# Twelve matmuls at equal addresses instead of six, in fewer pairs, and half of the output weights' sums a chunk earlier

## The chip, the cores and the metric

The kernel runs on one core of a Trainium2 chip. A core has five engines that run at their own pace and wait for one another by semaphores: TensorE (PE, the matmuls; PEld is its loading of the stationary operand), VectorE (DVE), ScalarE (ACT), GpSimd (POOL) and SyncE (SP), which here issues nearly all transfers, in the order in which the program names them. The metric is device time in microseconds of one execution. The kernel before took 809.94 us, the median of three runs (808.45, 809.94 and 810.32).

## The reference: what is computed

Linear attention without a mask, a normalisation, and a feed-forward layer with GELU, in float32:

```python
kv = np.einsum('bhsd,bhse->bhde', k, v)            # 8 batches, 8 heads, 576 tokens, 64 dims
out = np.einsum('bhsd,bhde->bhse', q, kv)
rms = np.sqrt(np.mean(out * out, axis=-1, keepdims=True) + 1e-06)
x = out / rms * g_norm                             # then 4608 tokens x 512
h = x @ w_in                                       # 512 x 2048
g = 0.5 * h * (1.0 + erf(h / sqrt(2)))
return g @ w_out                                   # 2048 x 512
```

The precision of float32 is reached with three matmuls per product on operands split in a high and a low part: high by high, high by low, low by high.

## The kernel before, in words

**Chunks.** The 4608 tokens are done in nine chunks of 512, numbered 0 to 8. The hidden dimension of 2048 is 16 blocks, or eight pairs `j` of blocks. While a chunk's feed-forward layer runs, the attention of the next chunk (projections, line 242; the sum of squares, line 274; scaling, lines 315 and 319) and the `kv` sums of the chunk after it (line 181) are woven in.

**Three ways to do the layers.** Chunks 0 and 1 multiply plainly: `layer1` (line 678) makes a block of `h` with 12 matmuls of 512 columns, then `layer2` (line 705) adds the block of the step before to the output with 12 more. From chunk 2 on the first layer, and from chunk 3 on the second layer too, use a Strassen-Winograd scheme: of each pair of blocks seven products are made instead of eight, from operands that are sums of quarter blocks. `product` (line 539) issues one of these, six matmuls of 256 columns at line 546. So the weights are needed as *sums*, split in high and low, and these are made once, during chunks 1 and 2, and written to a scratch tensor in device memory (`products_in`, `products_out`), from which later chunks read them back.

**Where the sums are made.** Chunk 1 runs in 16 steps `i`, one block each. In steps 1 to 11 VectorE forms the sums of the input weights (`combine`, lines 416 and 433; the low parts, line 449), between its share of GELU (`rest`, line 697: the low part of the block's activation, which `layer2` of the next step needs with its third matmul). In chunk 2, which runs over the eight pairs, GpSimd forms the sums of the output weights: `sum_out(j)` issues six tensor-tensor operations (through `add`, line 537), and one pair later `split_out(j)` splits the result, with two casts on ScalarE (line 1225) and two subtractions on VectorE (line 1226). Four transfers of 256 KB then write it out (`send`). A table, `SUMS`, says at which pair which sum is made. Within a pair of chunk 2, `layer1_pair` (line 550) lets VectorE copy the first product out of PSUM after products 0 and 1 (line 562) and add it to others (line 537, operands `h` and `w_in`); product 4, the 25th matmul of the pair, writes over the same place and so waits for that copy. After the pair come 24 plain matmuls of the second layer.

**Order.** Everything stands in an order written out by hand; each engine does its own instructions in that order, and a tile's next writer waits until all its readers are done. Tiles of 4 KB per partition are handed round by name (`take` and `free`).

**Fetching and addresses.** Six tiles (`RING`: `w_in0` to `w_in3`, `w_in10`, `w_in11`) form a ring into which `fetch` reads the weights' products, 512 KB (two products) at a time. All operand tiles start at the same remainder of 256 bytes. A fetched tile is put 192 bytes further on (`AWAY`, 48 float32) so that its address differs in that remainder from the operand that it is multiplied with. There are two exceptions, at *equal* remainders: the first product of each pair of the first layer (six matmuls, the first 256 KB of the keys `("in", j, 0)`, which are therefore fetched by two transfers, line 508), and the first tick of each second layer (12 matmuls).

**The first layer of chunks 3 to 8** is a run of 336 matmuls at line 546 in this order: 24 of pair 0 (products 0 to 3), 24 of pair 1, 18 of pair 0 (products 4 to 6), 24 of pair 2, 18 of pair 1, and so on, ending with 18 of pair 7. Attention matmuls stand in it after the 18 of pair 0 and of pair 1 (projections) and of pair 2 (line 274), and up to chunk 5 `kv` sums after those of pairs 3 and 6.

Of the kernel before, what the change touches and what calls it, by code (L numbers as in the profile page):

```python
# [8 lines left out]
F32 = mybir.dt.float32  # L9
# [28 lines left out]
def linear_attn_rms_gelu_ffn(  # L38
# [453 lines left out]
    def fetch(n):  # L492

        if n < len(queue):
            key = queue[n][1]
            i = RING[n % len(RING)]
            reused(i, F32R)
            away = [0 if key == ("out", *TICKS[0]) else AWAY] * 2
            if key == ("in", key[1], 0):
                away[0] = 0  # L500
            ring[n] = [kept[i][:, a * DM + away[a]:(a + 1) * DM + away[a]] for a in range(2)]
            if away[0] == away[1]:
                to = kept[i][:, away[0]:away[0] + 2 * DM]
                nc.sync.dma_start(out=to.bitcast(F32), in_=products[key])
            else:
                for a in range(2):
                    src = products[key][:, a * DM:(a + 1) * DM]
                    nc.sync.dma_start(out=ring[n][a].bitcast(F32), in_=src)

    def operand(c, key):  # L510
        at = c, key
        if at in place:
            return ring[place[at]]
        return resident[key][:, :DM], resident[key][:, DM:2 * DM]
# [24 lines left out]
    def product(at, j, k, out, first=False):  # L539
        *key, n = place_in(j, k)  # L540
        key = tuple(key)
        w, x = operand(at.c, key)[n], at.x[k]
# [417 lines left out]
    def spread_matmuls(c, i):  # L960
# [7 lines left out]
        if c and i == 14:  # L968
            sum_kv(c + 2, range(NP))
# [29 lines left out]

    def later(c, i):  # L1000
# [20 lines left out]

    order = list(range(3, len(weights)))
# [34 lines left out]
    for s in range(PLAIN * NF):  # L1057
# [6 lines left out]
        if c and i == 15:  # L1064
            split_kv(c + 2, range(NP))
# [38 lines left out]
    class Fast:  # L1104
# [44 lines left out]
        def matmuls(self, i):  # L1149
# [7 lines left out]
            for p in range(2):  # L1157
                hi, lo = (op[:, z * CH + p * HALF:z * CH + (p + 1) * HALF] for z in range(2))
                wh, wl = (w[p][:, m * HALF:(m + 1) * HALF] for m in range(2))
# [36 lines left out]

    wide, sent = {}, []

    def sum_out(j):

        eng = nc.gpsimd
        (name, whole), (of, s) = take(), take()
        for n in range(2):
            w = parts["out", 2 * j + n].bitcast(F32)
            add(whole[:, n * DM:(n + 1) * DM], w[:, HI], w[:, LO], eng=eng)
        a11, a21, a12, a22 = (whole[:, n * HALF:(n + 1) * HALF] for n in range(4))
        s1, s2, s3, s4 = (s[:, n * HALF:(n + 1) * HALF] for n in range(4))
        for o, x, op, y in (
            (s1, a21, ALU.add, a22), (s2, s1, ALU.subtract, a11),
            (s3, a11, ALU.subtract, a21), (s4, a12, ALU.subtract, s2),  # L1210
        ):
            add(o, x, y, op, eng)
        free.append(name)
        wide[j] = of, s

    def split_out(j, places=()):
        of, s = wide.pop(j)
        s = s.rearrange("p (h k n) -> p h k n", h=2, k=2)
        for h, ks in enumerate(((1, 2), (6, 5))):
            if places:  # L1220
                slot, t = places[h], block_tile(places[h], F32R)[:, :2 * DM]
            else:
                slot, t = take(F32R)
            t = piece(t)
            nc.scalar.copy(out=t[:, :, 0], in_=s[:, h])
            nc.vector.tensor_tensor(  # L1226
# [245 lines left out]
```

## Time and profile before

The profile is of one execution. It took 808.53 us, of which 806.7 us lie between its first and its last instruction (the span).

| | busy us | share of the span | instructions |
|---|---|---|---|
| PE | 793.6 | 98% | 6248 |
| PEld | 741.2 | 92% | 6248 |
| DVE | 564.7 | 70% | 1029 |
| ACT | 369.4 | 46% | 702 |
| POOL | 207.7 | 26% | 184 |

245.4 MB moved, 304 GB/s over the span. The mean granted TensorE clock is 0.998 of full speed. "Busy" of PE includes modelled ends of matmuls that overlap the next one, so a run of matmuls is better judged by the time from one piece of the chain to the next. By the chain, chunk 1 begins near 113 us, chunk 2 at 211.3 us, chunk 3 at 307.2 us; the first layers of chunks 4 and 8 begin at 396.8 and 726.1 us. A "step" below is one of chunk 1's 16 blocks, a "pair" one of the eight pairs of blocks in the later chunks.

### The profile page before, as it was taken

To read this page: it belongs to the slowest core of one execution; us is meant where nothing else is said; L and a number is where in the kernel's file an instruction comes from. 1 tells how busy PE (TensorE), PEld (TensorE's weight loads), DVE (VectorE), ACT (ScalarE), POOL (GpSimd) and SP (SyncE) were. 2 spreads that over 40 slices of the span, in tenths; PEclk is the share of its full clock that TensorE was granted. 3 is DMA by queue.
4 is the path that set the end of the run, shared out by engine and by line. 5 is a ranking of instruction groups with operands and counts; after the bars stand their busy time and mean duration, and the time that the engine had idled before them with its cause. 6 is when DMAs were issued, how large, how long until landed. Compare 5 with 4: busy or idle time off the path is not lost.

```text
span 806.7 us, 16291 instructions
## 1 busy us (share of the span) xinstructions
PE 793.6 (98%) x6248; PEld 741.2 (92%) x6248; DVE 564.7 (70%) x1029; ACT 369.4 (46%) x702; POOL 207.7 (26%) x184
## 2 busy tenths in 40 slices
PE   8999999999999989999999999999999999999998
PEld 6688888888998879999999999999999999999997
DVE  3999757678467873769467965786479648965683
ACT  2787534434352432547154635363445443532360
POOL 1000021102345922470038002810263016201200
PEclk9999999999999999999999999999999999999999
DMA  9991317998796899999989999989899989899984
GB/s 352 407 363 53 118 41 253 357 366 292 272 333 247 307 307 354 370 373 353 366 307 347 330 370 316 350 308 301 324 315 329 322 300 308 297 327 339 329 300 163
DMA packets 98577, 245.40 MB, mean 304 GB/s; under 512 B 9924, under 2 KB 31684, under 8 KB 98500
## 3 DMA queue, kind: packets, MB, share of 16 engines
q1 hardware_dynamic: 98496, 244.36, 85.4%
q8 instruction: 50, 0.82, 0.4%
q14 instruction: 27, 0.22, 0.1%
q10 hardware_dynamic: 4, 0.00, 0.0%
HBM read 205.52 MB, written 35.13 MB: 298 GB/s over the span
## 4 chain that ended last, share of the span: by engine, by line
PE 89%; DMA 6%; DVE 3%; issue 1%; POOL 0%; SPq 0%; ACT 0%; POOLq 0%
PE acc L1163 20%; PE acc L546 17%; PE acc L705 14%; PE h L546 13%; PE h L678 10%; PE a L1163 8%; PE a L242 3%; DMA w_in<-products_in 2%; PE a L181 2%; DMA kv_tail<-kv_tail 1%; PE h L670 1%; DMA w_out<-kv_main 1%; DMA q<-qT 1%; DMA products_out<-x 1%; DVE w_out L1226 1%
## 5 line engine op out<-in xcount | busy, mean ns | idle before, releaser
L705 PE MATMUL acc<-w_out,gh 128*128 128x512 f32 x312 | 97.7, 394 | 0.0
L678 PE MATMUL h<-x,w_in 128*128 128x512 f32 x360 | 87.3, 391 | 0.0
L229 POOL TENSOR_TENSOR ql<-q,qh 128x512 fp32r<-128x512 f32 x16 | 21.5, 1347 | 246.0 <-ACT qh L228 246.0
L678 PEld LDWEIGHTS h<-x,w_in 128*128 128x128 f32 x360 | 67.5, 188 | 14.6 <-POOL x L332 0.2
L546 PE MATMUL acc<-w_out,w_in 128*128 128x256 f32 x600 | 80.0, 280 | 0.2 <-DMA w_in<-products_in 0.2
L546 PEld LDWEIGHTS acc<-w_out,w_in 128*128 128x128 f32 x600 | 73.9, 188 | 0.6 <-issue 0.4
L1163 PE MATMUL acc<-w_in,w_out 128*128 128x256 f32 x576 | 71.6, 277 | 0.0
L705 PEld LDWEIGHTS acc<-w_out,gh 128*128 128x128 f32 x312 | 57.9, 188 | 12.6
L1163 PEld LDWEIGHTS acc<-w_in,w_out 128*128 128x128 f32 x576 | 68.3, 188 | 0.0
L705 PE MATMUL acc<-w_out,gl 128*128 128x512 f32 x156 | 61.4, 393 | 0.0
L691 ACT ACTIVATE gh<-h 128x512 fp32r<-128x512 f32 x39 | 23.3, 597 | 82.9 <-PE h L678 59.2
L546 PE MATMUL acc<-x,w_in 128*128 128x256 f32 x360 | 49.4, 279 | 0.0
L546 PE MATMUL h<-w_in,w_in 128*128 128x256 f32 x312 | 42.2, 286 | 6.7 <-DVE w_in L537 6.6
L1163 PE MATMUL acc<-w_in,x 128*128 128x256 f32 x384 | 48.0, 276 | 0.0
L546 PE MATMUL h<-w_out,w_in 128*128 128x256 f32 x360 | 47.8, 279 | 0.0
L697 DVE TENSOR_TENSOR gl<-h,gh 128x512 fp32r<-128x512 f32 x39 | 26.8, 687 | 29.9 <-ACT h L692 25.7
L546 PEld LDWEIGHTS h<-w_in,w_in 128*128 128x128 f32 x312 | 39.4, 194 | 7.7 <-DVE w_in L537 7.7
L1163 PEld LDWEIGHTS acc<-w_in,x 128*128 128x128 f32 x384 | 45.7, 188 | 0.0
L546 PEld LDWEIGHTS acc<-x,w_in 128*128 128x128 f32 x360 | 45.1, 188 | 0.2
L546 PEld LDWEIGHTS h<-w_out,w_in 128*128 128x128 f32 x360 | 44.4, 188 | 0.0
L1163 PE MATMUL acc<-w_in,w_in 128*128 128x256 f32 x336 | 42.2, 277 | 0.0
L546 PE MATMUL h<-x,w_in 128*128 128x256 f32 x312 | 42.0, 279 | 0.0
(281 smaller groups left out, 1784.2 us busy)
## 6 DMA issues: line engine op xcount, KB each, us to landing
w_in<-products_out SPq DMA_DIRECT2D x126, 512.0 KB, 5.4
w_in<-products_in SPq DMA_DIRECT2D x116, 512.0 KB, 5.3
w_in<-products_in SPq DMA_DIRECT2D x112, 256.0 KB, 5.2
kv_main<-kv_main SPq DMA_DIRECT2D x22, 512.0 KB, 6.5
products_in<-w_in SPq DMA_DIRECT2D x40, 256.0 KB, 5.4
w_in<-w_in SPq DMA_DIRECT2D x16, 512.0 KB, 10.2
w_out<-w_out SPq DMA_DIRECT2D x16, 512.0 KB, 10.2
q<-qT SPq DMA_DIRECT2D x15, 512.0 KB, 6.4
```

The source lines that it names most:

```text
L181: nc.tensor.matmul(out=ps[r, n * D:(n + 1) * D], lhsT=k[:, r], rhs=v[:, r], start=(j == 0), stop=(j == NJ),)
L229: eng.tensor_tensor(out=ql, in0=q, in1=qh.bitcast(F32), op=ALU.subtract)
L242: nc.tensor.matmul(out=ps[:, a:e], lhsT=w, rhs=x[:, a:e], start=(m == 0), stop=(m == 2))
L546: nc.tensor.matmul(out=out, lhsT=y, rhs=x[:, z, kb], start=first and kb + i == 0, stop=kb == 1 and i == 2, skip_group_check=True,)
L670: nc.tensor.matmul(out=h, lhsT=ws[i].bitcast(F32)[:, p * P:(p + 1) * P], rhs=at.o_all[:, p], start=(p == 0), stop=(p == NP - 1),)
L678: nc.tensor.matmul(out=h, lhsT=parts["in", i][:, w][:, p * P:(p + 1) * P], rhs=at.x[p][:, x], start=(m + p == 0), stop=(m == 2 and p == NP ...
L691: nc.scalar.activation(out=gh, in_=h, func=AF.Gelu)
L697: nc.vector.tensor_tensor(out=gl, in0=h, in1=gh.bitcast(F32), op=ALU.subtract)
L705: nc.tensor.matmul(out=ps, lhsT=x[:, ts], rhs=parts["out", i][:, w], start=(i == 0 and m == 0), stop=(m == 2 and (i == NF - 1 or (i, t) == ...
L1163: nc.tensor.matmul(out=ps[:, a * HALF:(a + 1) * HALF], lhsT=x[:, at], rhs=y, start=(k in (0, 2, 1) and n + p + a + m == 0), stop=(n == GRO ...
L1226: nc.vector.tensor_tensor(out=t[:, :, 1], in0=s[:, h], in1=t[:, :, 0].bitcast(F32), op=ALU.subtract)
```

## The change

The change has two halves.

**Addresses.** A fetched tile now lies at equal remainders as a whole (12 matmuls, products 0 and 1) or not at all, so each is read by a single transfer. Which ones do is in a new function, `aligned`: in chunk 2 the keys `("in", j, 0)` of all eight pairs; in chunks 3 to 5 those of pairs 0, 2, 3, 4, 5; in chunks 6 and 7 of pairs 0, 2, 3, 4; in chunk 8 of pair 0 alone. The first tick of each second layer stays as it was.

**Sums.** `sum_out` and `split_out` of output pairs 0 to 3 move from chunk 2 into chunk 1: `sum_out` at steps 6, 8, 10, 12 and `split_out` and `send` one step later, in tiles named by hand. Pairs 4 to 7 stay in chunk 2, at the pairs 1, 3, 5 and 7. With it three things of chunk 1 move: the loads of `kv` from step 13 to 12, the matmuls of the `kv` sums from step 14 to 15, and their split behind step 15's second layer. The tiles that stay resident are loaded in another order (`keep`).

```diff
-            away = [0 if key == ("out", *TICKS[0]) else AWAY] * 2
-            if key == ("in", key[1], 0):
-                away[0] = 0
-            ring[n] = [kept[i][:, a * DM + away[a]:(a + 1) * DM + away[a]] for a in range(2)]
-            if away[0] == away[1]:
-                to = kept[i][:, away[0]:away[0] + 2 * DM]
-                nc.sync.dma_start(out=to.bitcast(F32), in_=products[key])
-            else:
-                for a in range(2):
-                    src = products[key][:, a * DM:(a + 1) * DM]
-                    nc.sync.dma_start(out=ring[n][a].bitcast(F32), in_=src)
+            away = 0 if aligned(*queue[n]) else AWAY
+            ring[n] = kept[i][:, away:away + 2 * DM]
+            nc.sync.dma_start(out=ring[n].bitcast(F32), in_=products[key])
+
+    def aligned(c, key):
+
+        kind, j, k = key
+        if kind == "out":
+            return (j, k) == TICKS[0]
+        if k:
+            return False
+        n = 8 if c < FAST else 6 if c + 2 < B else 5 if c + 1 < NCH else 1
+        return j < n and (c < FAST or j != 1)
...
-        if c and i == 14:
+        if c and i == 15:
             sum_kv(c + 2, range(NP))
...
+    def sum_out(j, places=()):
+
+        eng = nc.gpsimd
+        if places:
+            name = of = None
+            whole, s = (block_tile(n, F32)[:, :2 * DM] for n in places)
+        else:
+            (name, whole), (of, s) = take(), take()
+        for n in range(2):
+            w = parts["out", 2 * j + n].bitcast(F32)
+            add(whole[:, n * DM:(n + 1) * DM], w[:, HI], w[:, LO], eng=eng)
+        a11, a21, a12, a22 = (whole[:, n * HALF:(n + 1) * HALF] for n in range(4))
+        s1, s2, s3, s4 = (s[:, n * HALF:(n + 1) * HALF] for n in range(4))
+        for o, x, op, y in (
+            (s1, a21, ALU.add, a22), (s2, s1, ALU.subtract, a11),
+            (s3, a11, ALU.subtract, a21), (s4, a12, ALU.subtract, s2),
+        ):
+            add(o, x, y, op, eng)
...
-        if i == 13:
-            for p in (2, 3):
-                load_kv(c + 2, p)
         if i == 15:
+            split_kv(c + 2, range(NP))
             attn[c + 2].load(1)
+        send()
         if i == 13:
             for n in range(4):
                 fetch(n)
...
+    EARLY = (6, 8, 10, 12)
...
+            if i == 12:
+                for p in (2, 3):
+                    load_kv(c + 2, p)
             n = 0 if not 1 <= i <= 11 else 2 if i in (1, 3, 5, 7, 11) else 1
             sum_weights(i, n, lambda: g.update({s: rest(*g[s])}))
+            if i in EARLY:
+                sum_out(EARLY.index(i), ("w_in2", "w_in3"))
+            elif i - 1 in EARLY:
+                n = EARLY.index(i - 1)
+                split_out(n, [f"w_in{m}" for m in ((4, 5), (6, 7), (4, 5), (6, 9))[n]])
             second_layer(s - 1)
             later(c, i)
...
-    SUMS = {0: (0,), 1: (1,), 2: (2,), 3: (3,), 4: (4, 5), 5: (6,), 7: (7,)}
+    SUMS = {1: (4,), 3: (5,), 5: (6,), 7: (7,)}
...
-            if 4 <= j:
-                keep(RESIDENT[(j - 2) % 4])
+            if j > 3:
+                keep(RESIDENT[j - 4])
```

Three places show how the instructions move. The first is GpSimd in chunk 1, from the step-7 split of the queries on (`ql`, line 229); `w_in` and `x` on the left are the tiles that take the sums, `w_out` the output weights. It is a piece of the difference, + for the change:

```order
-L229 TENSOR_TENSOR ql<-q,qh 128x512 x4
-L366 TENSOR_TENSOR x_2030<-o,x_2030 128x512
+L229 TENSOR_TENSOR ql<-q,qh 128x512 x3
+L537 TENSOR_TENSOR w_in_1710<-w_out_431 128x512
+L537 TENSOR_TENSOR w_in_1710<-w_out_479 128x512
+L537 TENSOR_TENSOR w_in_1711<-w_in_1710 128x256
+L537 TENSOR_TENSOR w_in_1711<-w_in_1711,w_in_1710 128x256
+L537 TENSOR_TENSOR w_in_1711<-w_in_1710 128x256
+L537 TENSOR_TENSOR w_in_1711<-w_in_1710,w_in_1711 128x256
```

The first of the four sums now stands ahead of GpSimd's fourth query split, the two next ones right behind that split and ahead of anything for step 12; before, GpSimd had nothing there.

The second is VectorE in chunk 1 at the passage from step 9 to step 10 (line 697 is step 9's `rest`, line 449 a low part of the input weights, lines 289 to 307 the inverse root of the next chunk's normalisation). With the change:

```order
L697 TENSOR_TENSOR gl<-h_1874,gh 128x512
L449 TENSOR_TENSOR w_in_1509<-w,w_in_1509 128x2x256
L1034 TENSOR_TENSOR w_in_1913<-w_in_1855,w_in_1913 128x2x256
L1034 TENSOR_TENSOR w_in_1916<-w_in_1855,w_in_1916 128x2x256
L289 TENSOR_SCALAR m<-a_1931 128x64
L292 TENSOR_SCALAR y<-m 128x64
L298 SCALAR_TENSOR_TENSOR t<-y 128x64
```

Before, line 449 was followed at once by line 289. The two rows of line 1034 are the subtractions of `split_out`; such a pair also stands behind steps 7, 11 and 13.

The third is VectorE in chunk 2 from the end of pair 5 to the copy in pair 6 (line 697: `rest` of pair 5; line 356: block sums of the next chunk's operand; line 562: the copy that product 4 of pair 6 waits for). Before:

```order
L697 TENSOR_TENSOR w_in_2438<-h_2930,w_in_2438 128x512
L1226 TENSOR_TENSOR x_3000<-x_2885,x_3000 128x2x256
L1226 TENSOR_TENSOR w_out_3003<-x_2885,w_out_3003 128x2x256
L1226 TENSOR_TENSOR w_out_3006<-x_2893,w_out_3006 128x2x256
L1226 TENSOR_TENSOR w_out_3009<-x_2893,w_out_3009 128x2x256
L356 TENSOR_TENSOR o<-o 128x2x256
L356 TENSOR_TENSOR w<-z,o 128x512
L356 TENSOR_TENSOR z<-o,w 128x512
L562 COPY w_in_2244<-h_3053 128x256
```

With the change:

```order
L697 TENSOR_TENSOR w_in_2506<-h_2947,w_in_2506 128x512
L356 TENSOR_TENSOR o<-o 128x2x256
L356 TENSOR_TENSOR w<-z,o 128x512
L356 TENSOR_TENSOR z<-o,w 128x512
L562 COPY w_in_2322<-h_3057 128x256
```

The four subtractions between the two pairs are gone: those of output pair 4 now stand in pair 2 of the chunk and those of output pair 5 in pair 4.

More of the change, by code (lines that the diff above doesn't have):

```diff
@@ L1158, in matmuls @@
                 hi, lo = (op[:, z * CH + p * HALF:z * CH + (p + 1) * HALF] for z in range(2))
-                wh, wl = (w[p][:, m * HALF:(m + 1) * HALF] for m in range(2))
+                wh, wl = (w[:, p * DM + m * HALF:p * DM + (m + 1) * HALF] for m in range(2))
                 for a in range(2):
@@ L1195, in after @@
                 )
[L1197 to L1226, printed above, removed]
-                out=t[:, :, 1], in0=s[:, h], in1=t[:, :, 0].bitcast(F32), op=ALU.subtract
-            )
-            sent.extend((place_out(j, k), t[:, a]) for a, k in enumerate(ks))
-            sent.append(slot)
-        free.append(of)
-    def send():
-        for x in sent:
-            if isinstance(x, str):
-                if x not in KEPT_IN:
-                    free.append(x)
-            else:
-                product_out(*x)
-        sent.clear()
     def ahead(c, j, place):
```

39 lines of the change are left out of this document (32 added, 7 removed).

## The prediction

> **What bounds the kernel now.** I read the chain of waits first, for the engine that sets the end, and then TensorE's own waits in chunk 2, 211 to 307 us:
>
> ```profile
> PE 89%; DMA 6%; DVE 3%; issue 1%; POOL 0%; SPq 0%; ACT 0%; POOLq 0%
> ...
> PE h L546 <- DVE w_in L537: 6.6, 4, 3.9
> ```
>
> TensorE sets the end, and nearly all that it waits for is VectorE in chunk 2: four waits, 6.6 us, the longest 3.9. What they cost with all that follows is read from the windows by pair; pairs 3 to 7 of chunk 2 are these (length, then busy time and count of PE, PEld, DVE, ACT, POOL, clock, DMA share, GB/s), and below them stands the chain's piece of `kv` matmuls that pair 3 holds too:
>
> ```profile
> 243.10:257.40 14.30, 13.44 (x148) 11.94 (x147) 10.42 (x19) 4.10 (x8) 7.13 (x8) 1.00 0.75 268
> 257.40:268.80 11.40, 10.65 (x67) 9.50 (x66) 8.49 (x17) 4.11 (x8) 11.09 (x12) 1.00 0.77 261
> 268.80:280.60 11.80, 10.71 (x67) 9.45 (x66) 10.23 (x16) 5.05 (x10) 11.49 (x11) 1.00 0.82 270
> 280.60:296.80 16.20, 12.27 (x68) 11.07 (x67) 12.84 (x19) 6.16 (x12) 4.83 (x4) 0.89 0.97 341
> 296.80:307.20 10.40, 10.40 (x67) 9.44 (x66) 5.29 (x11) 2.39 (x5) 2.34 (x2) 1.00 0.89 299
> ...
> 200.57 2.48 PE a L181 x80
> ```
>
> Pair 7 never waits and takes 10.40 us. Against it pair 3 loses 14.30 - 2.48 - 10.40 = 1.42, pair 4 1.00, pair 5 1.40 and pair 6 5.80 us: 9.62 us in all. Pair 6 loses more than its wait because the granted clock falls to 0.89 with it. The timeline tells why that pair waits (VectorE, then TensorE, start and length):
>
> ```profile
> 278.37 0.79 DVE L1226 TENSOR_TENSOR x<-x,x 128x512 fp32r<-128x512 f32 x1
> 279.09 3.53 DVE L1226 TENSOR_TENSOR w_out<-x,w_out 128x512 fp32r<-128x512 f32 x3
> 282.54 1.77 DVE L356 TENSOR_TENSOR o<-o 128x512 f32<-128x512 f32 x1
> ...
> 286.63 0.42 DVE L562 COPY w_in<-h 128x256 f32<-128x256 f32 x1
> ...
> 287.56 3.84 PE L546 MATMUL h<-w_in,w_in 128*128 128x256 f32 x18 [3.93 <-DVE w_in L537]
> ```
>
> The copy that product 4 waits for stands behind four subtractions of the output weights' split (4.3 us) and block sums that take 1.77 us each. Those are slow because GpSimd works beside them. The same is seen on the small operations of line 298: one alone, one beside GpSimd, and GpSimd's own:
>
> ```profile
> 242.90 0.23 DVE L298 SCALAR_TENSOR_TENSOR t<-t 128x64 f32<-128x64 f32 x1
> 243.16 0.73 DVE L298 SCALAR_TENSOR_TENSOR y<-t,y 128x64 f32<-128x64 f32 x1
> ...
> 243.07 0.74 POOL L537 TENSOR_TENSOR x<-w_out 128x256 f32<-128x256 f32 x1 [7.32 <-DMA products_out<-x]
> ```
>
> So a VectorE operation beside GpSimd takes as long as GpSimd's, and the two alternate. These are what the four waits are made of.
>
> **The change, part by part.** *Sums out of chunk 2.* Pair 6 loses its four subtractions; from 278.37 the block sums follow at once, and GpSimd has finished its sum by then, since the one for output pair 6 only waits for the one before it. At 0.7 us each (line 356 takes 0.7 us where GpSimd is idle) three of them end near 280.5, before products 0 and 1 do (some 1.4 us after the pair's start at 280.64): no wait, and no fall of the clock. In pair 3 the root's operations no longer meet a sum (two pairs earlier now): four at 0.73 to 0.79 become 0.23 us, about 2 us against a wait near 1. In pair 4 two subtractions less stand ahead of the copy, about 1.4 us against 1.0. In pair 5 the two subtractions stay, but GpSimd is through, which gives back more than 1.4 us (1.77 to 0.7 for one block sum alone). What hides the work that stays is TensorE's own 24 plain matmuls between the pairs. I take -9.0 of the 9.62. Bounds: -9.6, and -7.2 if pairs 3 and 4 keep their waits, as they would if GpSimd's scaling and not its sums held VectorE up.
>
> *Sums into chunk 1.* Four times six GpSimd operations, four times two casts on ScalarE, four times two subtractions on VectorE (1.4 to 1.6 us), 16 transfers of 256 KB. One sum is two of the first and four of the second kind:
>
> ```profile
> 208.37 2.54 POOL L537 TENSOR_TENSOR x<-w_out 128x512 f32<-128x512 f32 x2 [9.03 <-PE h L678]
> 210.99 0.74 POOL L537 TENSOR_TENSOR x<-x 128x256 f32<-128x256 f32 x1
> ```
>
> that is 2.54 + 4 x 0.74 = 5.5 us, on an engine that is nearly idle there. ScalarE has room too. VectorE is where it can hurt; these are steps 6-7, 8-9, 10-11, 12-13 and 14-15 of chunk 1:
>
> ```profile
> 151.30:163.30 12.00, 12.00 (x56) 9.87 (x54) 7.58 (x15) 5.35 (x10) 1.35 (x1) 1.00 1.02 341
> 163.30:175.40 12.10, 12.10 (x58) 10.01 (x56) 8.52 (x16) 4.31 (x8) 0.00 (x0) 1.00 1.07 372
> 175.40:186.60 11.20, 11.20 (x52) 9.09 (x51) 10.10 (x24) 3.75 (x7) 0.00 (x0) 1.00 1.04 371
> 186.60:197.70 11.10, 11.10 (x50) 9.03 (x49) 10.78 (x16) 6.42 (x12) 4.61 (x3) 1.00 0.68 214
> 197.70:211.30 13.60, 13.60 (x129) 11.31 (x128) 5.71 (x8) 4.18 (x9) 4.28 (x4) 1.00 0.82 321
> ```
>
> In steps 6 to 9 VectorE is idle for 8.0 of 24.1 us and takes the first two sums in. In steps 10 to 13 it is idle for 1.4 of 22.3. Its deadline is `rest` (line 697), whose result TensorE needs with the third of the next step's 12 second-layer matmuls, 0.47 us after their start (VectorE's rows of the root and of `rest` in steps 10 and 12, then the chain's pieces that need these):
>
> ```profile
> 175.63 0.22 DVE L289 TENSOR_SCALAR m<-a 128x64 f32<-128x64 f32 x1 [0.50 <-PE a L274]
> ...
> 177.67 0.23 DVE L298 SCALAR_TENSOR_TENSOR y<-t,y 128x64 f32<-128x64 f32 x1
> ...
> 180.03 0.68 DVE L697 TENSOR_TENSOR gl<-h,gh 128x512 fp32r<-128x512 f32 x1
> ...
> 191.22 0.68 DVE L697 TENSOR_TENSOR gl<-h,gh 128x512 fp32r<-128x512 f32 x1
> ...
> 183.95 2.80 PE acc L705 x12
> ...
> 195.09 2.74 PE acc L705 x12
> ```
>
> Step 10 has 183.95 + 0.47 - 180.71 = 3.7 us to spare. Two subtractions now stand ahead of the root (+1.5, of which the 0.50 us of waiting swallows a third), and the four short operations of GpSimd's third sum, which wait for just these subtractions, then run beside the root: 4 x (0.74 - 0.23) = 2.0 more. That makes 3.0 of 3.7: no wait yet. Step 12 has 195.09 + 0.47 - 191.90 = 3.7 to spare and inherits the 3.0, as nothing idle lies between, plus step 11's subtractions (1.5), plus about 0.7 of the fourth sum beside the scaling: 5.2, so TensorE waits 1.5 us. Step 13's block sums meet the rest of that sum, and with the `kv` matmuls moved behind step 15 its deadline comes 2.5 us earlier: another 0.9 by the same reckoning. I take 2.4 for this; behind step 15 VectorE has 7.9 us idle and catches up.
>
> The transfers go into a queue that is full: over 140 to 190 us the first row below, and the second is the fetch of the weights for chunk 2 (first start, 195.3 us), the third their time to land (minimum, median, maximum):
>
> ```profile
> DMA packets 13656, 17.92 MB, mean 358 GB/s; under 512 B 1040, under 2 KB 9836, under 8 KB 13653
> ...
> L508 SPq DMA_DIRECT2D w_in<-products_in x112: 319/320/1193, 195.3 to 749.7; - x112
> ...
> DMA to landing us min/median/max: 2.9/5.2/7.7
> ```
>
> 16 x 262 KB = 4.2 MB is 11.7 us at that rate; behind 186.6 the shares 0.68 and 0.82 leave 3.6 + 2.4 = 6.0 us free, so the first fetches come some 5.7 us later than now. They land near 201 us and are needed from 211.3: covered, but the last four transfers stand ahead of the fetches in SP's queue and wait for a late VectorE, so I add 0.8. Together +3.2. Bounds: 0, and +8.7 if both sums in steps 10 to 13 hold VectorE up for their whole time (2 x 5.5 + 2 x 1.5 - 1.4 - 3.7, about).
>
> *Addresses.* The chain's pieces of chunk 8's first layer, where no attention interferes, and the passage to the second layer in chunk 4:
>
> ```profile
> 726.10 2.82 PE h L546 x24
> ...
> 731.75 2.12 PE h L546 x18
> ...
> 753.06 2.76 PE h L546 x24
> ...
> 760.62 2.04 PE h L546 x18
> ...
> 764.70 1.32 PE acc L1163 x11
> ...
> 440.01 2.32 PE acc L546 x18
> 442.33 21.92 PE acc L1163 x192
> ```
>
> 18 matmuls with no product at equal remainders take 2.04 us late in the layer (113.3 ns each) and 2.12 (117.8) early: there are two paces. 24 with one such product take 2.76, so the six at equal remainders take 120 ns: 0.04 us dearer than fast ones. Chunk 8 goes from 726.10 to 764.70, 38.60 us for 336 matmuls; at the fast pace it were 38.08. All slow would lose 1.5 us a chunk. Nothing but the equal products distinguishes the place where chunk 8 turns fast, so I read them as what can turn the pace, and six often fail: pairs 0 and 1 hold one each and stay slow. Twelve stand ahead of each second layer, and there 192 matmuls take 21.92 (21.76 at the fast pace), even behind a slow first layer. If chunks 3 to 7 lose 1.0 us each (between chunk 8's 0.52 and 1.5), 5.5 us are lost now. With twelve that always work, 23 pairs would pay 0.08 each, 1.9 us: -3.6. With twelve that never work, all is slow: 9.0 us, +3.5. In the second layer the fetched tile is the streamed operand and here the loaded one, so I trust that row for two cases in three: -1.2.
>
> The Trainium skill ("SBUF — State Buffer", "Who interferes with whom") gives TensorE two independent read ports, one for the streamed operand and one for weight loads, and has it wait on nobody. By that, remainders could not matter and this term would be 0; the two prices for 24 matmuls above speak against it.
>
> *The rest* I cost at nothing: one transfer instead of two for a fetch saves SP 0.3 us in a queue that TensorE does not wait for here, at the price that product 0 waits for 512 KB; the order of `keep` and step 15's split lie beside pair 0.
>
> **The sum** against the profiled execution's 808.53: -9.0 + 3.2 - 1.2 = -7.0, so 801.5. That execution lies 1.4 below the median of the runs, so for a median 809.9 - 7.0 = 802.9 us. A difference under 0.2% (1.6 us) cannot be told from none here.
>
> **The rivals**, each as a median. *VectorE fits and the pace always turns*: -9.6 + 0 - 3.6, 796.7. For it: the first two sums do fit; against it: 1.4 us idle in steps 10 to 13. *Addresses do nothing*: -9.0 + 3.2, 804.1; this is the page's rule. *Twelve do not turn the pace*: -9.0 + 3.2 + 3.5, 807.6; for it, pairs 0 and 1 above. *Half the waits stay in chunk 2*: pairs 3 and 4 keep theirs and a part of pair 6, about -7 + 3.2 - 1.2, 804.9. *VectorE's lag in chunk 1 takes over*: if every VectorE operation meets GpSimd, four sums cost 4 x (5.5 + 1.5) = 28 us, less 9.4 idle in steps 6 to 13 and 3.7 to spare: 15 us, so 809.9 - 9.0 + 15 - 1.2 = 814.7, slower. It decides from a lag of about 13 us on. Against it: half of VectorE's operations there read PSUM, and `rest` took 0.68 in all rows.
>
> **How the numbers follow.** Forecast 0.45 (its own range 800 to 806), then 0.15, 0.12, 0.13, 0.07 and 0.08. The range 797.0 to 808.5 leaves out the slower rival and the ends of the fastest. Faster: all but the last and a part of the third rival, 0.87; same 0.05; slower 0.08.
>
> **What would show it.** Right: no wait of TensorE on line 537 over 1 us in pairs 3 to 6, the clock at 1.00 there, and those pairs near 10.4 us; a wait for `gl` of line 697 near steps 12 and 13 of chunk 1, where now there is none; 24 matmuls with twelve equal ones at 2.80 and 18 behind them at 2.04. Wrong: waits of 5 us or more in chunk 1, waits for fetches at the start of chunk 2, or 2.12 throughout.

## The result, and the profile after

The changed kernel took 801.23 us (median of four runs, 800.68 to 801.69) against 809.20 for the kernel before beside it: a ratio of 0.9903, with a 95% interval of 0.9882 to 0.9923. The prediction was 802.9. Its profiled execution took 801.69 us, 6.84 less than that of the kernel before; a second profile of the same kernel (the first experiment) took 800.75. Executions that fell into a slower state are left out of all ratios; they took 814.81, 977.56 and 2799.17 us. By the starts of the chunks' first matmuls the difference lies here:

| us | before | changed | difference | second profile |
|---|---|---|---|---|
| up to chunk 1 | 113.58 | 113.38 | -0.20 | -0.33 |
| chunk 1 | 97.73 | 99.95 | +2.22 | +2.36 |
| chunk 2 | 95.91 | 87.05 | -8.86 | -8.66 |
| chunk 3 | 89.46 | 89.02 | -0.44 | -1.00 |
| chunk 4 | 83.73 | 84.25 | +0.52 | +0.51 |
| chunk 5 | 83.99 | 84.85 | +0.86 | +0.61 |
| chunk 6 | 81.31 | 81.28 | -0.03 | -0.37 |
| chunk 7 | 80.23 | 79.79 | -0.44 | -0.44 |
| chunk 8, to the end of its second layer | 76.94 | 76.48 | -0.46 | -0.46 |

The sums decide it, as forecast: what changes is chunk 2, less what chunk 1 pays. Chunks 3 to 8, where only the addresses differ, give 0.0 us in this profile and -1.15 us in the second. These are TensorE's waits in the changed kernel, and pairs 3 to 7 of its chunk 2 (columns as in the prediction):

```profile
PE acc L705 <- DVE gl L697: 1.6, 1, 1.6
...
PE acc L546 <- DMA w_in<-products_in: 0.6, 1, 0.6
...
PE h L546 <- DMA w_in<-products_in: 0.4, 1, 0.4
...
245.21:258.31 13.10, 13.10 (x148) 11.82 (x147) 8.20 (x19) 3.53 (x7) 5.48 (x4) 1.00 0.71 239
258.31:268.60 10.29, 10.29 (x67) 9.34 (x66) 7.77 (x15) 3.75 (x7) 9.23 (x11) 1.00 0.60 209
268.60:279.07 10.47, 10.47 (x68) 9.39 (x66) 8.73 (x15) 4.26 (x8) 1.73 (x2) 1.00 0.76 231
279.07:290.08 11.01, 10.63 (x68) 9.49 (x67) 8.63 (x16) 4.69 (x9) 1.33 (x1) 1.00 1.00 396
290.08:300.37 10.29, 10.29 (x67) 9.34 (x66) 5.38 (x11) 2.48 (x5) 1.46 (x2) 1.00 0.78 252
```

The four waits on VectorE in chunk 2 are gone and the clock stays at 1.00. Less the 2.48 us of `kv` matmuls in pair 3, pairs 3 to 6 take 10.62, 10.29, 10.47 and 11.01. Pair 6 now waits for a fetch (0.4), with the DMA share at 1.00. (In the second profile it waits 0.58 us, put down to VectorE; but the fetch landed there at 282.49 us, just as late as VectorE's operation, and in the first profile the matmul started before that operation ended.) Against the clean 10.40 of the kernel before they lose 0.79 in all; it was 9.62. The new wait, 1.6 us for `rest` (line 697), is in chunk 1. There VectorE, GpSimd and TensorE are:

```profile
176.74 0.21 DVE L289 TENSOR_SCALAR m<-a 128x64 f32<-128x64 f32 x1
176.99 0.77 DVE L292 TENSOR_SCALAR y<-m 128x64 int32<-128x64 int32 x1
177.79 0.81 DVE L298 SCALAR_TENSOR_TENSOR t<-y 128x64 f32<-128x64 f32 x1
...
180.81 0.23 DVE L298 SCALAR_TENSOR_TENSOR y<-t,y 128x64 f32<-128x64 f32 x1
...
194.63 0.68 DVE L697 TENSOR_TENSOR gl<-h,gh 128x512 fp32r<-128x512 f32 x1
...
195.82 3.44 POOL L537 TENSOR_TENSOR w_in<-w_out 128x512 f32<-128x512 f32 x2
...
198.15 1.67 DVE L356 TENSOR_TENSOR o<-o 128x512 f32<-128x512 f32 x1
199.74 1.23 DVE L356 TENSOR_TENSOR w<-z,o 128x512 f32<-128x512 f32 x1
200.89 1.21 DVE L366 TENSOR_TENSOR w_in<-o,w_in 128x512 fp32r<-128x512 f32 x1
202.02 0.68 DVE L697 TENSOR_TENSOR gl<-h,gh 128x512 fp32r<-128x512 f32 x1
...
202.75 0.50 PE L705 MATMUL acc<-w_out,gl 128*128 128x512 f32 x1 [1.63 <-DVE gl L697]
```

The root of step 10 runs beside GpSimd's third sum (0.77 and 0.81 us where it took 0.20 and 0.22) and ends 3.14 us later than before (180.81 against 177.67). Step 12's `rest` is 3.4 us later than before, and TensorE barely waits. Then the fourth sum's two long operations run beside step 13's block sums, which take 1.67, 1.23 and 1.21 us (0.69, 0.68, 0.68 before), and step 13's `rest` is 5.7 us later: there TensorE waits for 1.63 us. Steps 6 to 9, ahead of all this, were meant to take the first two sums in without trouble. They do, but barely (steps 6-7 and 8-9; VectorE's busy time is the third one, 11.29 and 11.96):

```profile
151.00:163.00 12.00, 12.00 (x56) 9.89 (x55) 11.29 (x17) 5.99 (x12) 6.63 (x6) 1.00 1.04 344
163.00:175.10 12.10, 12.10 (x58) 10.02 (x56) 11.96 (x18) 5.97 (x12) 7.04 (x6) 1.00 1.06 366
```

VectorE was idle for 8.0 us there and is now for 0.9.

In chunks 4 and 5 the first layers are faster than before and the second ones slower. This is the second layer of chunk 4, in groups of 12 matmuls, one tick each, and the VectorE operation that makes the seventh tick's low half:

```profile
441.13 1.52 PE L1221 MATMUL acc<-w_in,w_out 128*128 128x256 f32 x12
442.49 1.63 PE L1221 MATMUL acc<-w_in,x 128*128 128x256 f32 x12
443.95 1.58 PE L1221 MATMUL acc<-w_out,w_in 128*128 128x256 f32 x12
445.37 1.58 PE L1221 MATMUL acc<-w_in,w_in 128*128 128x256 f32 x12
...
441.93 0.68 DVE L1199 TENSOR_TENSOR x<-w_out,x 128x512 fp32r<-128x512 f32 x1
...
434.39 22.45 PE acc L1221 x192
```

Until 442.49 the ticks start 1.36 us apart (113.3 ns a matmul). VectorE's operand is done at 442.61; the third matmul of the tick, at 442.72, comes 66 ns late, and from then on the ticks are 1.41 us apart (117.8 ns) to the end of the layer: 192 matmuls take 22.45 us, where the prediction's row of the kernel before has 21.92. Over the whole layer it is 39.41 us instead of 38.24, and the same happens in chunk 5. The stall, too short for the list of waits, is at the same place in both profiles of this kernel.

### The profile page after: what moved, and what is told of

Same layout as the page of the kernel before. It is cut to its first block, busy times and chain, and to the rows that moved or that the text cites. A ratio compares the mean times of both kernels' runs of the same rounds, so it can differ in the third digit from the quotient of the medians.

```text
span 799.9 us, 16183 instructions
## 1 busy us (share of the span) xinstructions
PE 791.7 (99%) x6248; PEld 739.4 (92%) x6248; DVE 573.3 (72%) x1029; ACT 369.7 (46%) x702; POOL 210.6 (26%) x184
## 4 chain that ended last, share of the span: by engine, by line
PE 88%; DMA 5%; DVE 4%; SPq 1%; issue 1%; ACT 0%; DVEq 0%
PE acc L1221 21%; PE acc L546 17%; PE h L546 15%; PE acc L705 12%; PE a L1221 8%; PE h L678 7%; PE a L242 3%; PE a L181 3%; DMA products_in<-w_in 2%; DMA w_in<-products_in 2%; SPq L405 1%; PE h L670 1%; PE h L790 1%; DVE w L433 1%; DVE z L416 1%
## 5 line engine op out<-in xcount | busy, mean ns | idle before, releaser
L1221 PE MATMUL acc<-w_in,w_out 128*128 128x256 f32 x696 | 86.1, 278 | 0.0
L1221 PEld LDWEIGHTS acc<-w_in,w_out 128*128 128x128 f32 x696 | 82.7, 188 | 0.0
L678 PEld LDWEIGHTS h<-x,w_in 128*128 128x128 f32 x360 | 67.5, 188 | 14.5 <-POOL x L332 0.2
L546 PE MATMUL acc<-w_out,w_in 128*128 128x256 f32 x450 | 61.0, 280 | 0.8 <-DMA w_in<-products_in 0.6
L546 PEld LDWEIGHTS acc<-w_out,w_in 128*128 128x128 f32 x450 | 55.6, 188 | 1.4 <-ACT w_out L602 0.8
L546 PE MATMUL h<-w_in,w_in 128*128 128x256 f32 x402 | 52.1, 277 | 0.4 <-DMA w_in<-products_in 0.4
L546 PEld LDWEIGHTS h<-w_in,w_in 128*128 128x128 f32 x402 | 48.7, 188 | 0.7 <-issue 0.5
L537 DVE TENSOR_TENSOR gl<-acc,gh 128x256 f32<-128x256 f32 (+1 forms) x66 | 29.3, 444 | 16.9 <-ACT gh L583 13.6
L265 DVE TRANSPOSE_TENSOR_REDUCE part<-sq 128x16 f32<-128x512 f32 x33 | 23.4, 709 | 23.1 <-ACT sq L252 23.1
L546 PEld LDWEIGHTS h<-x,w_in 128*128 128x128 f32 x312 | 39.2, 189 | 0.7
L583 ACT COPY gh<-h 128x256 f32<-128x256 f32 x18 | 6.8, 376 | 68.2 <-PE h L546 68.2
```

The source lines that it names most:

```text
L265: nc.vector.tensor_reduce(out=self.part[:, p, :], in_=sq.rearrange("p (b d) -> p b d", d=BLK), op=ALU.add, axis=AX.X, apply_transpose=True,)
L537: eng.tensor_tensor(out=out, in0=x, in1=y, op=op)
L546: nc.tensor.matmul(out=out, lhsT=y, rhs=x[:, z, kb], start=first and kb + i == 0, stop=kb == 1 and i == 2, skip_group_check=True,)
L678: nc.tensor.matmul(out=h, lhsT=parts["in", i][:, w][:, p * P:(p + 1) * P], rhs=at.x[p][:, x], start=(m + p == 0), stop=(m == 2 and p == NP ...
L1221: nc.tensor.matmul(out=ps[:, a * HALF:(a + 1) * HALF], lhsT=x[:, at], rhs=y, start=(k in (0, 2, 1) and n + p + a + m == 0), stop=(n == GRO ...
```

## Experiments

The figures on layers below are the time of a layer's 336 matmuls, each counted to the start of TensorE's next instruction, from the traces:

| us | first layers, chunks 4 to 8 | of these 7 and 8 | second layer of 4, of 5 |
|---|---|---|---|
| before | 196.51 | 39.13, 38.60 | 38.24, 38.18 |
| changed, first profile | 194.61 | 38.72, 38.14 | 39.41, 39.41 |
| changed, second profile | 194.03 | 38.72, 38.14 | 39.41, 39.41 |
| addresses alone | 194.09 | 38.72, 38.14 | 38.25, 38.28 |
| sums alone | 196.50 | 39.13, 38.60 | 38.22, 38.18 |
| a second equal tick | 194.01 | 38.72, 38.14 | 38.43, 38.44 |
| no equal products | 195.30 | 38.17, 38.08 | 38.17, 38.17 |
| twelve equal in every pair | 195.57 | 39.04, 38.70 | 38.18, 38.18 |
| fourth sum moved | 194.09 | 38.72, 38.14 | 38.26, 38.28 |
| fourth sum moved, ninth tick equal | 194.09 | 38.72, 38.14 | 38.36, 38.37 |
| fourth sum moved, 7 and 8 without | 193.51 | 38.17, 38.08 | 39.40, 38.27 |

### The two halves apart

The changed kernel once more, for comparison. 

> The changed kernel once more, as the measure for the three kernels beside it. Both theories: 0.990 of the kernel before, some 8 us. If the second layers of chunks 4 and 5 lose 1.2 us each by a chance that differs from execution to execution, this profile can show 38.2 us where the first one showed 39.4; if the stall of 65 ns there is part of the order of work, it shows 39.4 again in both.

The address half alone: the kernel before with the new `fetch` and `aligned`, and the sums where they were.

> The address half alone. The prediction on record: -1.2 us (1.2 shorter than before), with 1.0 us less in the first layers of chunks 3 to 7. The theory from the trace of the changed kernel: twelve matmuls turn the pace in most pairs, the first layers of chunks 3 to 8 get 2.2 us shorter (0.3 to 0.65 each, chunk 6 none), the pairs of chunk 2 about 0.1 each, and a second layer that then comes earlier than VectorE's operands can fall into the slow pace behind a short stall at its seventh tick, 1.2 us each: -3.0 us if none falls, -0.6 if two do. Addresses do nothing: 0, and 336 matmuls of a first layer take the same within 0.1 us.

The same once more, a single run, for a trace:

> The address half alone once more, for a trace at full clock. First layers of chunks 3 to 8 near 39.2, 39.0, 39.1, 39.05, 38.7, 38.1 us as in the changed kernel if the sums play no part in them; pairs 3 to 6 of chunk 2 with the waits of the kernel before. Second layers of chunks 4 and 5: 39.4 us if the earlier arrival of TensorE at the seventh tick is what makes the stall there, 38.2 if the moved sums have a part in it.

The sums alone: the changed kernel with the old rule,

```diff
-            away = 0 if aligned(*queue[n]) else AWAY
+            away = [0 if key == ("out", *TICKS[0]) else AWAY] * 2
+            if key == ("in", key[1], 0):
+                away[0] = 0
```

> The half with the sums alone, with six matmuls at equal remainders in each pair as before. The prediction's terms: -9.0 + 3.2 = -5.8 us. From the trace of the changed kernel: chunk 1 +2.2, chunk 2 about -8.4 (a clean pair 10.40 as before and not 10.29), first layers of chunks 3 to 8 as before: -6.2 us, of which the second layers lose nothing as long as they start no earlier against VectorE. Rival, the whole gain is the sums and the addresses take a little away: -7 or more.

Measured: the changed kernel again 0.9895 of the kernel before (0.9875 to 0.9914), the addresses alone 0.9979 (0.9966 to 0.9992), which is -1.7 us (-2.8 to -0.6), the sums alone 0.9914 (0.9898 to 0.9930), -7.0 us. Both halves are worth something, and their sum, -8.7, is what the two give together (-8.5). The address half is two things at once, the addresses and one transfer where there were two; no run takes them apart, but the layer times in the table show where its gain lies. The trace of the addresses alone (805.38 us) has the first layers of the changed kernel without its sums. Its second layers did not fall slow, though they stall at the same tick, so the moved sums are not needed for the stall, and the stall alone does not decide what follows.

### Does an equal product bring the pace back?

The changed kernel, with the ninth tick of the second layers at equal remainders too:

```diff
-            return (j, k) == TICKS[0]
+            return (j, k) in (TICKS[0], TICKS[8])
```

> The changed kernel with one more tick at equal remainders in each second layer, the ninth, that is two ticks behind the place where chunks 4 and 5 fell slow. If the pace is a state that a stall sets and equal products reset: the second layers of chunks 4 and 5 take 38.4 instead of 39.4 us (the ticks 7 and 8 slow, 0.15 us, and 0.08 for the tick itself), the others 0.08 more: -2.0 + 0.3 = -1.7 us against the changed kernel. If the slow matmuls there come from something else that lasts (traffic, VectorE beside it): they stay at 118 ns behind the ninth tick and the kernel takes +0.5 us.

Measured 0.9881 (0.9865 to 0.9897), 1.1 us under the changed kernel's 0.9895 with intervals that overlap. The trace shows what the times leave open. Chunk 4, ticks 7 to 11:

```profile
443.40 1.62 PE L1221 MATMUL acc<-w_in,x 128*128 128x256 f32 x12
444.86 1.58 PE L1221 MATMUL acc<-w_out,w_in 128*128 128x256 f32 x12
446.27 1.60 PE L1221 MATMUL acc<-w_in,w_in 128*128 128x256 f32 x12
447.71 1.54 PE L1221 MATMUL acc<-w_in,w_out 128*128 128x256 f32 x12
449.08 2.88 PE L1221 MATMUL acc<-w_in,x 128*128 128x256 f32 x24
```

The stall is at 443.4, the next tick is slow (1.41 us to the following start), the equal one starts at 446.27, and two ticks on the 24 matmuls are back at 113.3 ns each. The layer takes 38.43 us; 38.4 was expected. So in these two layers the pace is a state that outlasts the stall, and twelve equal products bring it back.

### Without equal products, and with them everywhere

```diff
-        if k:
-            return False
-        n = 8 if c < FAST else 6 if c + 2 < B else 5 if c + 1 < NCH else 1
-        return j < n and (c < FAST or j != 1)
+        return False
```

> The changed kernel with no product of any first layer at equal remainders (the first tick of each second layer stays). If equal products are what turns TensorE to 113.3 ns: every first layer of chunks 3 to 8 stays at 118 ns wherever it starts slow, 336 x 4.5 ns = 1.5 us a layer against the 0.1 to 0.9 us that it loses now, so +1.0 a chunk, +6 us, and the pairs of chunk 2 take 10.45 to 10.5 (+0.2 each, +1.3): +7 us, 808 in all, so the whole gain over the kernel before is gone. If the pace turns by itself and equal products only cost 7 ns each: -0.08 for 23 pairs, -1.9 us.

and the same with `return True` for every pair:

> The changed kernel with twelve equal matmuls in every pair of every first layer, 24 pairs more. By the price of 0.08 us for a run of twelve: +1.9 us, less what chunks 5 and 6 save if the second pair turns them fast (0.3 each): +1.3. So half or more of what the first layers gained (2.3 us) would come from leaving equal products out, not from having twelve. If the pairs left out lose their pace now and then and twelve would bring it back: 0 or below.

Measured 0.9891 (0.9874 to 0.9907) and 0.9888 (0.9873 to 0.9903): neither differs from the changed kernel. For the first one my theory asked for +7 us. The layer times show what it missed. In chunks 3 to 6, where the attention matmuls come in twelves and not in sixes as in chunk 7, the layers without equal products are slower, by 0.5 to 0.8 us each against the second profile, as the theory has it. But chunks 7 and 8 are fast throughout. This is chunk 8 from its start on, without equal products, and below it the same in the second profile of the changed kernel (chain of waits; the product's line is 543 in the first):

```profile
718.53 2.72 PE h L543 x24
721.25 2.72 PE acc L543 x24
723.98 2.04 PE h L543 x18
...
718.78 2.78 PE h L546 x24
721.56 2.72 PE acc L546 x24
724.28 2.04 PE h L546 x18
```

All 336 take 38.08 us, the time that the prediction had worked out for a layer at the fast pace, and no equal product stands in it. The second layer before had ended fast, and nothing disturbed it. In the kernel before it was the first product at equal remainders that turned this layer slow:

```profile
724.58 1.52 PE L1163 MATMUL a<-w_out,w_out 128*128 128x256 f32 x12
725.94 1.57 PE L546 MATMUL h<-w_out,w_in 128*128 128x256 f32 x12
727.34 0.87 PE L546 MATMUL h<-x,w_in 128*128 128x256 f32 x6
728.05 0.87 PE L546 MATMUL h<-w_out,w_in 128*128 128x256 f32 x6
```

(To the next start: 1.36 us for the 12 ahead of it, 1.40 for its own 12, and 0.71 and 0.70 for the sixes behind, where 0.68 is fast.) Chunk 8 starts slow in the three other kernels with six there as well, and fast in both without any. Twelve can do the same harm, as chunk 7 shows, behind its first six attention matmuls (line 242). The second profile of the changed kernel, with twelve equal ones in these 42, and below it the kernel without:

```profile
647.90 4.97 PE acc L546 x42
...
648.15 4.76 PE acc L543 x42
```

The 18 matmuls ahead take 2.04 us in both, so TensorE comes fast to this place. Without equal products 42 matmuls go on at 113.3 ns. Twelve equal ones at 120 ns would add 0.08 us; the 0.21 that they add means that the other 30 went slow. All seven traces with twelve in that pair show the same. So equal products turn the pace in both directions: slow to fast in many places where a layer is slow, and fast to slow in some where it is fast, six at the start of chunk 8 and twelve in pair 2 of chunk 7. Nor are they the only thing that turns it: in chunks 3 and 5 of the kernel without them, the 18 matmuls ahead of the two at line 274 take 2.12 us and the next 18 take 2.04. And the second layers of chunks 4 and 5 do not stall in these two kernels, which gives 2.5 us back. Sums over the chunks: without equal products +0.5 in chunk 2, about +2.6 in the first layers of 3 to 6, -0.6 in 7 and 8, -2.5 in the second layers, 0 in all.

With twelve in every pair, the 24 pairs more cost 1.80 us in the first layers of chunks 3 to 8 (235.05 against 233.25 in the second profile), 0.075 each: the forecast price was 0.08. In chunk 3 the kernel before waits for fetches too, so the gain is better split in chunks 4 to 8: of 2.5 us there, 1.5 come from leaving pairs out (195.57 to 194.03) and 0.9 from twelve for six (196.51 to 195.57). 1.80 us over 288 matmuls are 6.3 ns each. By the rule of the Trainium skill that the prediction set against it ("SBUF — State Buffer", "Who interferes with whom": TensorE waits on nobody) this would be 0; the measurement decides.

### What made VectorE late in chunk 2

The kernel before without the subtractions of the split (ScalarE writes a copy in their place, so a second copy of the sums stands where their low parts belong), and then the kernel before without GpSimd's sums (a fill with zeros in their place):

```diff
-            nc.vector.tensor_tensor(
-                out=t[:, :, 1], in0=s[:, h], in1=t[:, :, 0].bitcast(F32), op=ALU.subtract
-            )
+            nc.scalar.copy(out=t[:, :, 1], in_=s[:, h])
```

> The kernel before with the subtractions of the output weights' split left out on VectorE: ScalarE writes a copy in the place of each low part, so the output weights' sums are not split rightly; GpSimd's sums stay. By the prediction: pairs 4, 5 and 6 of chunk 2 lose their waits (1.0 + 1.4 + 5.8), pair 3, whose wait is made by the root beside GpSimd's sum, keeps its 1.4: -8 us. If GpSimd alone makes VectorE late: pair 6 still has its block sums at 1.77 us, and half of the 9.6 stays: -3 to -5 us.

```diff
-        for n in range(2):
-            w = parts["out", 2 * j + n].bitcast(F32)
-            add(whole[:, n * DM:(n + 1) * DM], w[:, HI], w[:, LO], eng=eng)
...
-            add(o, x, y, op, eng)
+        eng.memset(s, 0.0)
```

> The kernel before with the output weights' sums on GpSimd left out in chunk 2: one fill with zeros stands for the six operations, so the sums are wrong; VectorE's subtractions stay. By the prediction's reading of the stalls: pair 3 loses its 1.4, pair 5 its block sum at 1.77, pair 6 has four subtractions at 0.7 (2.8 instead of 4.3 us) and a block sum at 0.7 and keeps a wait of about 1.3 us without a fall of the clock: -6.5 us. If the subtractions alone are the cause: pairs 4 to 6 stay, -1.5 us.

Measured 0.9941 (0.9918 to 0.9964), -4.8 us, and 0.9930 (0.9904 to 0.9955), -5.7 us. Pairs 3 to 7 without subtractions, then without GpSimd's sums:

```profile
242.91:256.12 13.21, 13.21 (x147) 11.92 (x146) 7.25 (x14) 5.52 (x11) 8.32 (x8) 1.00 0.81 289
256.12:266.55 10.43, 10.43 (x67) 9.46 (x66) 7.80 (x15) 4.49 (x9) 10.12 (x12) 1.00 0.75 248
266.55:277.10 10.55, 10.55 (x67) 9.44 (x66) 8.29 (x13) 5.49 (x11) 10.24 (x11) 1.00 0.92 303
277.10:287.72 10.62, 10.58 (x67) 9.45 (x66) 6.84 (x13) 6.03 (x12) 4.81 (x4) 1.00 1.00 388
287.72:300.77 13.05, 10.71 (x68) 9.52 (x66) 5.38 (x11) 5.59 (x10) 1.27 (x1) 1.00 0.93 323
```

```profile
242.58:255.79 13.21, 13.21 (x148) 11.92 (x146) 8.62 (x20) 4.11 (x8) 4.75 (x5) 1.00 0.82 283
255.79:266.91 11.12, 10.69 (x68) 9.52 (x66) 8.17 (x17) 4.21 (x8) 1.90 (x3) 1.00 0.76 263
266.91:277.46 10.55, 10.55 (x68) 9.44 (x66) 8.24 (x16) 4.67 (x9) 0.00 (x0) 1.00 0.82 261
277.46:289.12 11.66, 10.60 (x68) 9.45 (x67) 8.31 (x15) 5.20 (x10) 3.00 (x2) 1.00 1.03 393
289.12:300.94 11.82, 10.69 (x67) 9.51 (x66) 6.83 (x14) 3.94 (x7) 1.27 (x1) 1.00 0.98 332
```

Without the subtractions all four waits are gone, pair 3's too, which I had expected to stay: 8.9 us over pairs 3 to 6. That the whole gains only 4.8 has other reasons: pair 7 waits 2.3 us for VectorE (ScalarE's copies and casts there wait for transfers out of the tiles that they write, and VectorE behind them), chunk 3 is 1.3 us longer, and the second layer of chunk 4 fell slow (39.40). Without GpSimd's sums pair 6 keeps 11.66 - 10.40 = 1.26 us, and the clock stays at 1.00: the expectation was 1.3. Pair 4 keeps 0.7. So it takes both, subtractions and operations that GpSimd slows; in pairs 3 and 5 either one gone is enough. Pair 7 is 1.4 us longer in the second kernel for the same reason as in the first: ScalarE's casts wait 1.60 and 1.11 us for transfers, VectorE waits for the casts, and TensorE 1.13 us for VectorE.

### Where chunk 1's loss comes from, and a better kernel

The changed kernel with the fourth sum at pair 0 of chunk 2:

```diff
-    EARLY = (6, 8, 10, 12)
+    EARLY = (6, 8, 10)
...
-    SUMS = {1: (4,), 3: (5,), 5: (6,), 7: (7,)}
+    SUMS = {0: (3,), 1: (4,), 3: (5,), 5: (6,), 7: (7,)}
```

> The changed kernel with the fourth output sum not at step 12 of chunk 1 but at pair 0 of chunk 2, where GpSimd is idle. If the sum beside steps 12 and 13 is what makes VectorE late there (two waits of TensorE, 0.23 and 1.63 us): both are gone, chunk 1 is 1.9 us shorter, and pairs 0 to 2 of chunk 2 stay at 9.12, 12.2 and 10.57: -1.9 us against the changed kernel. If VectorE's lag comes from the subtractions and sums of steps 6 to 11, or from the kv sums that now stand behind step 15: the waits stay, 0 us; and if pair 1 of chunk 2 now waits for VectorE as pairs 3 to 6 did before: +1 us.

with the ninth tick at equal remainders in chunks 3 to 5 besides (`or c + 2 < B and (j, k) == TICKS[8]`):

> The fourth sum at pair 0 of chunk 2, and the ninth tick of the second layer at equal remainders in chunks 3 to 5 alone. If both causes are as thought: -1.9 and -2.0 + 0.1, 3.8 us under the changed kernel, 0.985 to 0.986 of the kernel before. If the one or the other gain is given back: -2.

and, instead of that tick, with no equal products in the first layers of chunks 7 and 8 (`if k or c + 2 >= NCH: return False`):

> The kernel with the fourth sum at pair 0 of chunk 2, and no equal remainders in the first layers of chunks 7 and 8. If equal products turn a fast TensorE slow at the start of an undisturbed layer, as chunks 7 and 8 of the kernel without any equal products suggest: their first layers take 38.17 and 38.08 us instead of 38.72 and 38.14, -0.6 us against the kernel with the fourth sum moved alone, 797.0. If those layers were fast for another reason (no stall in the second layers before): 38.7 again in chunk 7, 0 us.

Measured 0.9851 (0.9836 to 0.9865), 0.9854 (0.9840 to 0.9869) and 0.9865 (0.9850 to 0.9880), medians of 797.63, 797.82 and 797.79 us: all three beat the changed kernel by 2.4 to 3.6 us, though the third one's interval touches the changed kernel's, and they can't be told from one another. Chunk 1 takes 99.08, 97.99 and 98.05 us, 1.0 to 2.1 less than in the changed kernel's second profile; pairs 0 to 2 of chunk 2 keep their time. In the first of them one wait is left at step 12, in that execution only:

```profile
PE acc L705 <- DVE gl L697: 1.2, 1, 1.2
...
198.70 0.69 DVE L356 TENSOR_TENSOR o<-o 128x512 f32<-128x512 f32 x1
```

The block sums of step 13 are back at 0.69 us, all but the first, and TensorE does not wait at step 13 in any of the three. The fourth sum was the cause of the 1.63 us. The rest of the first kernel's gain, which I had not expected, is in the second layers of chunks 4 and 5 (38.26 and 38.28): they stall there at the seventh tick as before, and recover by themselves within five matmuls. In the second kernel they recover too, so its ninth tick had nothing to mend and cost its 0.08: its time was forecast rightly, for a wrong reason. In the third, chunks 7 and 8 take 38.17 and 38.08 as expected, which is 0.6 us won, but the second layer of chunk 4 fell slow once more (39.40), although up to chunk 7 this kernel is the same program as the first: whether such a stall turns the pace differs between executions of one order of work.

## Why the prediction was right, and where it was not

**The time** (802.9 forecast, 801.23 measured; -7.0 from profile to profile forecast, -6.84 and -7.78 measured) came out of terms of which the largest was nearly right and two were off in opposite directions by about a microsecond in the profile: chunk 1 paid 2.2 where 3.2 was forecast, and the addresses gave 0.0 in chunks 3 to 8 where 1.2 was.

**Sums out of chunk 2:** -9.0 forecast, -8.9 measured for the chunk. With the sums alone chunk 2 takes 87.69 us, 8.2 less than before; the other 0.6 come only with the addresses changed too. No wait on VectorE is left in pairs 3 to 6, and the clock holds. That both the subtractions and GpSimd's work beside VectorE make the waits was shown by taking each away; that pair 3's wait was made by GpSimd alone was wrong, since it goes without the subtractions too. Two details of pair 6 failed without harm: its block sums still take 1.79 and 1.67 us, not 0.7, because GpSimd's two operations of line 366 run beside them (from 277.34 us, 3.06 us long), and a wait for a fetch (0.4 us) came. In the kernel before, too, it was line 366 (from 282.02 us, 3.41 us long) and not the output sum that ran beside the block sums of 1.77 us; the prediction had taken that for the sum's doing.

**Sums into chunk 1:** +3.2 forecast, +2.2 measured (+2.6 with the sums alone). The lag of step 10 was right to 0.1 us (3.0 against 3.14), and so were its parts: the root starts 1.1 us later and takes 2.0 us longer. The step that failed is the one behind it: the lag at step 12 was 3.4 and not 5.2. By step 11's `rest` it had shrunk to 2.7 (187.77 us against 185.11); the subtractions then added 1.2, and a scaling operation that GpSimd had slowed to 1.15 us took 0.69. The fourth sum met step 13's block sums and not the scaling, so the wait came at step 13: 0.23 at step 12 and 1.63 at step 13, not 1.5 and 0.9. The 0.8 us for fetches was not paid, but nearly: SyncE's queue, and the time to land of the fetches up to 240 us (minimum, median, maximum), read

```profile
203.32 3.22 SPq L405 DMA_DIRECT2D products_out<-w_in  x4
206.59 1.90 SPq L500 DMA_DIRECT2D w_in<-products_in  x4
...
DMA to landing us min/median/max: 5.0/6.2/9.6
```

The last four writes of sums do stand ahead of the fetches, and the first fetch is issued 11.3 us later than before, not 5.7. It landed at 211.75 (5.16 us), 1.6 us ahead of the matmul at 213.32 that needs it; in the kernel before it had 10 us.

**Addresses:** -1.2 forecast; -1.7 alone (-2.8 to -0.6), -1.5 as the difference of the changed kernel and the sums alone. The size was right by luck of the mixture. The mechanism, that equal products turn TensorE fast and twelve do it more surely than six, holds where attention has made the layer slow, and failed in chunks 7 and 8: chunk 8's loss of 0.52, one of the bounds for "5.5 us are lost now", was made by the equal products themselves. (The count of pairs that pay for twelve is 24, not 23, which changes the sum by 0.1 us.) The row of 2.76 us for 24 matmuls was read rightly as a price of 0.04 for six. And the sum had no term for the second layers, which I took as fast because their first tick had always turned them: it did so in all profiles, but a stall of 66 ns six ticks later undid it in chunks 4 and 5. That costs 2.4 us, against the 2.2 us (first profile) or 3.5 us (second) that the first layers of chunks 3 to 8 gain.

**The rivals.** "Addresses do nothing" (804.1) describes the first profile by its outcome, but not its cause, and the measured -1.7 (-2.8 to -0.6) excludes it for the address half as a whole. "VectorE's lag takes over" would have needed 13 us; it was 2. "Twelve do not turn the pace" and "half the waits stay" fell with the first layers' gain and with pairs 3 to 6. "The pace always turns" is wrong in pairs 2 and 3 of chunk 7, which are slow behind their twelve in both profiles, and in the first profile at the start of chunks 5 and 6. Where twelve do turn it, the marks are as forecast: 24 matmuls with twelve equal ones take 2.78 us at the start of chunk 8 (2.80 forecast), and the 18 behind 2.04.

## What to carry to other kernels

When two engines share the work, count what stands ahead of the one operation that the bound engine waits for, and ask which neighbour makes it slow; here 1.4 to 4 us of VectorE's queue cost 9.6 us, and work that moved to a place with 3.7 us of slack cost 2. A gain in one stage makes the next start earlier against its suppliers: look there for the stall that eats it. And compare layers with the same work in several chunks, with and without the suspected cause, before taking a cure for harmless: the slow start of chunk 8 was the cure's own, and so were the slow pairs of chunk 7.

## What was not expected of the hardware

TensorE has two paces for these matmuls, 113.3 and 117.8 ns, at a granted clock of 1.00 in both, and stays in either for hundreds of matmuls. A stall shorter than one matmul can change it. At the seventh tick of a second layer, 19 stalls can be seen in the 13 traces at hand (the gap of the starts there, 113 ns without a stall): three of 143 to 158 ns recovered within five matmuls; of ten from 170 to 186 ns eight turned the layer slow to its end or to the next equal tick; six of 192 to 207 ns recovered again. So a longer stall is not a worse one. What decides it stays open. Twelve matmuls at equal remainders stand at the start of every second layer, and it was fast behind them in every trace. In the first layers they do not always help, and in pair 2 of chunk 7 they turn a fast TensorE slow.
